# First attention batch loaded in fp32 by the SP and ACT queues and cast on chip, weights behind it, more banks for the last feed-forward products

## The chip, the cores and the metric

One Trainium2 chip, one NeuronCore. The metric is the device time of one execution in microseconds (us). In the profile PE is TensorE (PEld its weight loads), DVE is VectorE, ACT is ScalarE, POOL is GpSimd and SP is SyncE. Transfers issued by SP or ACT are called hardware-queue transfers here (the profile's `hardware_dynamic`), those issued by POOL software-queue transfers (`software_dynamic`). Only the latter convert fp32 to fp16 on the way in this kernel.

## What is computed

Sparse causal attention over 8 batches of 8 heads with 576 positions of width 64, then a feed-forward layer over all 4608 tokens.

```python
scores = scale * np.matmul(q, k.transpose(0, 1, 3, 2))
rel = pos[:, None] - pos[None, :]
mask_local = (rel >= 0) & (rel < stride)                                   # heads 0 to 3, stride 32
mask_strided = (rel >= 0) & (pos[None, :] % stride == pos[:, None] % stride)  # heads 4 to 7
scores = np.where(masks[None, :, :, :], scores, -1000000000.0)
attn = softmax(scores)
x = np.matmul(attn, v)            # -> (4608 tokens, 512)
h = x @ w_in                      # (512, 2048)
g = s * np.maximum(h, 0.0) ** 2 + b
out = g @ w_out                   # (2048, 512), fp32
...
```

## The kernel before

**Attention.** A batch is four head pairs: m = 0, 1 are local heads (6 tiles of 96 rows), m = 2, 3 strided heads (8 tiles of 72 rows). A pair goes through PE transposes of q and k (`ps_t`), copies out of PSUM by ACT or DVE (`qD_loc`, `kT_loc`, `qD_str`, `kTs`), score products (`ps_s`), the exponential on ACT (`pt`), the mask on DVE, the products with v (`ps_a`), a reciprocal and a multiplication on DVE (`rec`, `x_nat`), transposes back and a copy into `xT`. Only one PSUM bank serves `ps_a` (`AB = 1`), so the av groups of a batch (four local, eight strided) follow one another through PE, `rec` and `x_nat`. Local q and k are first regrouped by `pair_heads` (four DVE copies into `qp` and `kp`, L217).

**Feed-forward.** Tokens go in 9 blocks T of 512. F1 (L448) takes 4 products into `ps_f`, two banks; ACT writes `u` (L463), DVE squares it into `gT` (L467). F2 (L484) takes 16 products for 128 tokens into one bank (`F2B = 1`), DVE evicts (`o`, L495), SP stores. A block is 64 F1 and 64 F2 products. Ahead of the first F2 product stand 16 bias products (L506, `bcs`), which need `w_out`.

**Order.** A planner (`Plan`) emits all instructions in one order. It has a clock of its own, prices for each step (37 ns for a small PE step, 213.5 for a large one) and for each follow-up on ACT ("A") and DVE ("V"), and due times for transfers, which are constants in the code. What it believes ready it emits; on the chip every engine then executes its instructions strictly in that order, so an instruction emitted ahead of its data holds all behind it on that engine.

**Loads before.** Everything comes over POOL's queue, cast on the way: q, k, v of batch 0, `w_in` in four pieces, q, k, v of batch 1, `w_out` in one piece, then q and k of batch 2 and so on. The due times are those of the lines below; `fetch` is called for batch b + 2 when the last q or k transpose of batch b has been emitted.

```python
fetch(0, 10000.0)                     # L523: due 10 us
arrive([("in", "vl", 0), ("in", "vs", 0)], 22500.0)
fetch(1, 38000.0)
arrive([("w_out",)], 61000.0)         # L533
fetch(b + 2, plan.t + 12000.0)        # L542
```

POOL has 8 semaphores for transfers in turn, so a ninth waits for the landing of the first. In local v, both sides of a row are 64 elements (256 bytes in memory); rows of q, k and the weights are 1.5 to 2 KB.

Of the kernel before, what the change touches and what calls it, by code (L numbers as in the profile page):

```python
# [9 lines left out]
FP16 = mybir.dt.float16  # L10
FP32 = mybir.dt.float32
# [95 lines left out]
def kernel(  # L107
# [71 lines left out]
    nc.sync.dma_start(out=ident, in_=h_ident.ap())  # L179
    nc.sync.dma_start(out=mask_loc, in_=h_mloc.ap())  # L180
    nc.sync.dma_start(out=mask_str, in_=h_mstr.ap())
    nc.sync.dma_start(out=s_sb, in_=moe_s.to_broadcast([128, 1]))
    nc.sync.dma_start(out=b_sb, in_=moe_b.to_broadcast([128, 1]))
    nc.vector.memset(ones16, 1.0)
# [4 lines left out]
    for i in range(2):  # L189
        nc.vector.memset(kT_loc[i][:, 0:LPAD], 0.0)  # L190
        nc.vector.memset(qD_loc[i], 0.0)
        nc.vector.memset(qD_str[i], 0.0)

    loaded = {}

    def load_qk(b):
        t = {}
        for name, src in (("q", q), ("k", k)):
            tl = inp.tile([LQ, 4, LT * D], FP16, tag=name + "l", name=name + "l")
            nc.gpsimd.dma_start(  # L200
                out=tl, in_=src[b, 0:4].rearrange("h (p j) d -> p h (j d)", j=LT))
            t[name + "l"] = tl
        for name, src in (("q", q), ("k", k)):
            ts = inp.tile([SQ, 4, ST * D], FP16, tag=name + "s", name=name + "s")
            nc.gpsimd.dma_start(  # L205
                out=ts, in_=src[b, 4:8].rearrange("h (p j) d -> p h (j d)", j=ST))
            t[name + "s"] = ts
        loaded[b] = t

    paired = {}  # L210

    def pair_heads(b):
        for name in ("q", "k"):
            t = inp.tile([LQ, 2, LT, 2 * D], FP16, tag=name + "p", name=name + "p")
            src = loaded[b][name + "l"].rearrange("p (m e) (j d) -> p m e j d", e=2, d=D)
            for mm in range(2):
                nc.vector.tensor_copy(  # L217
                    out=t[:, mm].rearrange("p j (e d) -> p e j d", e=2), in_=src[:, mm])
            paired[b, name] = t

    def load_v(b):
        vl, vs = v_loc[b % NV], v_str[b % NV]
        for h in range(4):
            nc.gpsimd.dma_start(  # L224
                out=vl[LPAD:128, h, 0, 0:D], in_=v[b, h, 0:LQ, :])
# [14 lines left out]
    def load_w_out():  # L240
        nc.gpsimd.dma_start(
            out=w_out_sb, in_=moe_w_out.rearrange("(ft p) m -> p ft m", p=128))
# [3 lines left out]

    def copy_on(eng, **kw):
        (nc.scalar.copy if eng == "A" else nc.vector.tensor_copy)(**kw)  # L248

    def pair_steps(b, m):  # L250
# [10 lines left out]
        def trans(name, j, group):  # L261
            def f():
                if j == 0:
# [3 lines left out]
                       loaded[b][name + sfx][:, 2 * mm + j // 4,  # L267
                                             (j % 4) * 128:(j % 4) * 128 + 128])
# [3 lines left out]
            s = Step(f, 37, needs=[("in", name + sfx, b)], group=group if j == 0 else None)  # L272
            if j == nt - 1:
                key = ("t", name, id_)
                s.keys = [key]
                if name == "q":
# [15 lines left out]
                    s.posts = [([key], {"A": 620, "V": 750}, half(e), [("q", e, id_)])  # L292
# [3 lines left out]
                else:  # L296
# [9 lines left out]
                    s.posts = [([key], {"A": 640, "V": 750}, g, [("k", id_), group])]  # L306
# [9 lines left out]
        def score(i, group):  # L316
# [3 lines left out]
            def f():  # L320
                if i % per_s == 0:
                    st["s", g] = psum.tile([128, 3 * 2 * SQ], FP32, tag="s", bufs=SB, name="ps_s")
# [43 lines left out]
        def av(e, j, group):  # L366
# [10 lines left out]
            s = Step(f, 37, needs=[("p", id_, p_of(e, j)[0]), ("in", "v" + sfx, b)],  # L377
                     group=group if j % per == 0 else None)
            if j % per == per - 1:
# [10 lines left out]
                def mu(eng):  # L390
# [6 lines left out]
                           ([("r", id_, e, j)], {"V": 150 + 1.1 * 64 * per}, mu,  # L397
# [10 lines left out]
        def xtrans(j, group):  # L408
# [10 lines left out]
            if j == nt - 1:  # L419
# [10 lines left out]
                s.posts = [([key], {"A": 640, "V": 750}, g, [("xT", b, m), group])]  # L430
# [47 lines left out]
    def ff2(T, ts, ft, group):  # L478
        def f():
            if T == 0 and ts == 0 and ft == 0:  # L480
                emit_bcs()
            if ft == 0:
                gts["o"] = psum.tile([128, PS], FP32, tag="f2", bufs=F2B, name="ps_f2")
# [4 lines left out]
        s = Step(f, 213.5, needs=[("g", T, ft), ("w_out",)], group=group if ft == 0 else None)  # L488
        if ft == NFT - 1:
# [3 lines left out]
            def ev(eng):  # L493
                o = op.tile([128, DM], FP32, tag="o", name="o")
                nc.vector.scalar_tensor_tensor(  # L495
                    out=o, in0=gts["o"], scalar=s_sb[:, 0:1], in1=bcs,
# [3 lines left out]
            s.posts = [([key], {"V": 760}, ev, [group])]  # L500
        return s

    def emit_bcs():
        ps = psum.tile([128, PS], FP32, tag="f2", bufs=F2B, name="ps_f2")
        for ft in range(NFT):
            nc.tensor.matmul(out=ps, lhsT=ones16, rhs=w_out_sb[:, ft, :],  # L506
                             start=(ft == 0), stop=(ft == NFT - 1))
        nc.scalar.activation(out=bcs, in_=ps, func=AF.Copy, scale=b_sb)
# [6 lines left out]
    def fetch(b, at):  # L515

        load_qk(b)
        arrive([("in", "ql0", b), ("in", "kl0", b)], at)
        arrive([("in", "qs", b), ("in", "ks", b)], at + 4500)
        plan.post([("in", "ql0", b), ("in", "kl0", b)], {"V": 2000},  # L520
# [121 lines left out]
```

## Time and profile before

| | us |
|---|---|
| median of 3 runs (407.05 to 408.32) | 407.07 |
| the profiled execution | 407.57 |
| its span, first to last instruction | 405.5 |
| PE busy in it | 338.8 |
| DVE, ACT, POOL busy | 198.0, 183.9, 101.5 |

The span is 2.07 us shorter than the execution that it belongs to. PE's busy time is that of a pipelined engine: 84% does not mean that 84% of its peak is reached, since products overlap: four large ones take 0.86 us in the chain at 2.4 GHz and up to 1.86 us at 1.2 GHz. The page's 40 slices are 10.1 us each.

### The profile page before, as it was taken

The page shows a single profiled execution, that of the slowest core. Times are in us where ns is not written, and L with a number is a line of the kernel's source. Part 1 is how long each engine was busy: PE and PEld are TensorE (multiplying, and loading weights), DVE is VectorE, ACT ScalarE, POOL GpSimd, SP SyncE. Part 2 cuts the span into 40 slices and gives each one's busy share as a digit, 9 for nine tenths or more (in the row PEclk, how much of TensorE's full clock was granted, in tenths as well). Part 3 has the DMA queues.
Part 4 walks back from the last instruction along what each step waited for, and adds up shares of the span by engine and source line. Part 5 has one row for each costly group of instructions (what it writes and reads, how often), then busy time and mean ns, then how long its engine had stood idle before and what let it go on. Part 6 is the DMA issues. An engine that isn't in the chain of part 4 may idle for free.

```text
span 405.5 us, 6425 instructions
## 1 busy us (share of the span) xinstructions
PE 338.8 (84%) x2512; PEld 187.8 (46%) x2512; DVE 198.0 (49%) x545; ACT 183.9 (45%) x338; POOL 101.5 (25%) x137
## 2 busy tenths in 40 slices
PE   0665505967999799979997999799899999999884
PEld 0553302644455455545554555455555544444331
DVE  3554006774255646664665466456756643242311
ACT  1631204852355645564656555555655533332200
POOL 6744906354006500650064017100000000000000
PEclk9999955985999999989999999999999999999999
DMA  7999999798016940991099029400100001010111
GB/s 98 97 203 151 88 204 119 78 90 85 6 53 92 96 76 27 121 110 34 26 120 118 26 47 109 51 27 39 41 26 27 27 26 53 27 53 26 47 58 53
DMA packets 72514, 28.95 MB, mean 71 GB/s; under 512 B 53028, under 2 KB 67876, under 8 KB 72484
## 3 DMA queue, kind: packets, MB, share of 16 engines
q0 software_dynamic: 66640, 19.04, 51.0%
q1 hardware_dynamic: 5844, 9.51, 6.3%
q8 instruction: 19, 0.31, 0.3%
q14 instruction: 11, 0.09, 0.1%
HBM read 38.08 MB, written 9.44 MB: 117 GB/s over the span
## 4 chain that ended last, share of the span: by engine, by line
PE 73%; DMA 11%; ACT 5%; DVE 5%; POOL 4%; issue 2%; POOLq 0%; ACTq 0%
PE ps_f L484 30%; PE ps_f L448 29%; DMA kl<-in_k_dram 4%; DMA ks<-in_k_dram 4%; PE ps_a L373 4%; PE ps_t L269 3%; PE ps_s L324 3%; DMA qs<-in_q_dram 3%; ACT qD_loc L248 2%; PE ps_t L412 2%; DVE qD_loc L248 2%; DVE x_nat L391 1%; PE ps_f L506 1%; ACT pt L337 1%; DVE o L495 1%
## 5 line engine op out<-in xcount | busy, mean ns | idle before, releaser
L448 PE MATMUL ps_f<-xT,w_in_sb 128*128 128x512 f16 x576 | 165.5, 392 | 20.7 <-ACT u L463 19.0
L484 PE MATMUL ps_f<-w_out_sb,gT 128*128 128x512 f16 x576 | 156.2, 381 | 4.4 <-DVE o L495 3.6
L463 ACT ACTIVATE u<-ps_f 128x512 f16<-128x512 f32 x144 | 86.0, 598 | 101.6 <-PE ps_f L448 71.2
L467 DVE TENSOR_TENSOR gT<-u 128x512 f16<-128x512 f16 x144 | 60.1, 419 | 82.0 <-ACT u L463 81.2
L448 PEld LDWEIGHTS <-w_in_sb 128*128 128x128 f16 x576 | 56.0, 100 | 69.2 <-issue 24.6
L484 PEld LDWEIGHTS <-gT 128*128 128x128 f16 x576 | 55.9, 99 | 58.0 <-issue 7.6
L373 PEld LDWEIGHTS <-pt 72*72 72x72 f16 (+1 forms) x448 | 41.0, 128 | 25.9 <-DVE x_nat L391 15.1
L337 ACT ACTIVATE pt<-ps_s 128x384 f16<-128x384 f32 (+2 forms) x96 | 44.3, 488 | 18.3 <-PE ps_s L324 18.1
L391 DVE TENSOR_TENSOR x_nat<-ps_a,rec 72x256 f16<-72x256 f32 (+1 forms) x96 | 44.4, 463 | 2.3
L387 DVE RECIPROCAL rec<-ps_a 72x4 f32<-72x4 f32 (+1 forms) x96 | 17.5, 182 | 50.6 <-PE ps_a L373 49.7
L373 PE MATMUL ps_a<-v_str,pt 72*72 72x65 f16 x256 | 32.8, 207 | 7.3 <-DVE x_nat L391 7.2
L248 ACT COPY xT<-ps_t 128x576 f16<-128x576 f16 x30 | 19.2, 639 | 38.1 <-PE ps_t L412 37.9
L495 DVE SCALAR_TENSOR_TENSOR o<-ps_f,s_sb,bcs 128x512 f32<-128x512 f32 x36 | 26.9, 746 | 15.9 <-PE ps_f L484 15.6
L230 POOL DMA_DIRECT2D v_str<-in_v_dram x32 | 29.4, 917 | 18.6 <-PE ps_s L324 5.8
L229 POOL DMA_DIRECT2D v_loc<-in_v_dram x32 | 28.6, 894 | 16.5 <-DMA v_loc<-in_v_dram 8.9
L412 PE MATMUL ps_t<-ident,x_nat 72*128 72x72 f16 (+1 forms) x224 | 26.9, 211 | 4.2 <-DVE x_nat L391 4.1
L205 POOL DMA_DIRECT2D qs<-in_q_dram x8 | 5.9, 743 | 97.6 <-PE ps_t L269 97.6
L324 PE MATMUL ps_s<-qD_str,kTs 128*72 128x144 f16 x128 | 23.5, 238 | 1.1 <-ACT kTs L248 0.8
L324 PE MATMUL ps_s<-qD_loc,kT_loc 128*128 128x192 f16 x96 | 18.7, 274 | 5.6 <-ACT kT_loc L248 4.3
L373 PE MATMUL ps_a<-v_loc,pt 128*96 128x65 f16 x192 | 21.3, 213 | 1.2 <-DVE x_nat L391 1.2
L412 PEld LDWEIGHTS <-x_nat 72*128 72x128 f16 (+1 forms) x224 | 16.3, 104 | 11.2 <-DVE x_nat L391 6.8
L224 POOL DMA_DIRECT2D v_loc<-in_v_dram x32 | 17.4, 543 | 14.4 <-DMA w_out_sb<-in_moe_w_out_dram 10.4
(43 smaller groups left out, 246.2 us busy)
## 6 DMA issues: line engine op xcount, KB each, us to landing
out_dram<-o SPq DMA_DIRECT2D x36, 256.0 KB, 2.0
v_loc<-in_v_dram POOLq DMA_DIRECT2D x32, 80.0 KB, 4.7
ql<-in_q_dram POOLq DMA_DIRECT2D x8, 288.0 KB, 5.2
kl<-in_k_dram POOLq DMA_DIRECT2D x8, 288.0 KB, 6.7
qs<-in_q_dram POOLq DMA_DIRECT2D x8, 288.0 KB, 5.0
ks<-in_k_dram POOLq DMA_DIRECT2D x8, 288.0 KB, 8.0
v_str<-in_v_dram POOLq DMA_DIRECT2D x32, 72.0 KB, 4.0
w_in_sb<-in_moe_w_in_dram POOLq DMA_DIRECT2D x4, 512.0 KB, 9.2
```

The costliest lines, as they stand in the source:

```text
L230: nc.gpsimd.dma_start(out=vs[:, h, :, 0:D], in_=v[b, 4 + h].rearrange("(p j) d -> p j d", j=ST))
L248: (nc.scalar.copy if eng == "A" else nc.vector.tensor_copy)(**kw)
L324: nc.tensor.matmul(out=st["s", g][0:nk, c:c + 2 * nq], lhsT=st["k"][:, i * nq:i * nq + nk], rhs=st["q"][:, i].rearrange("d e c -> d (e c)"))
L337: nc.scalar.activation(out=pt[0:nk, 0:2 * n].rearrange("k t c -> k (t c)"), in_=st["s", g][0:nk, 0:2 * n * nq], func=AF.Exp, scale=scale)
L373: nc.tensor.matmul(out=st["a"][0:nq, j % per, :], lhsT=st["pt", g][0:nk, i, :], rhs=vt[0:nk, 2 * mm + e, j, :])
L391: nc.vector.tensor_tensor(out=st["x"][:, j0:j0 + per, 64 * e:64 * e + 64], in0=st["pa", e, j][0:nq, 0:per, 0:D], in1=st["rec", e, j][0:nq, ...
L412: nc.tensor.matmul(out=st["px"][:, nq * j:nq * j + nq], lhsT=st["x"][:, j, :], rhs=ident[0:nq, 0:nq], is_transpose=True)
L448: nc.tensor.matmul(out=gts["h"], lhsT=w_in_sb[:, ct, ft * 128:(ft + 1) * 128], rhs=xT[ct][:, tok0:tok0 + PS], start=(ct == 0), stop=(ct == 3))
L463: nc.scalar.activation(out=gts["u", T, ft], in_=h, func=AF.Relu)
L467: nc.vector.tensor_tensor(out=gts[T][:, ft, :], in0=u, in1=u, op=ALU.mult)
L484: nc.tensor.matmul(out=gts["o"], lhsT=gts[T][:, ft, ts * 128:(ts + 1) * 128], rhs=w_out_sb[:, ft, :], start=(ft == 0), stop=(ft == NFT - 1))
L495: nc.vector.scalar_tensor_tensor(out=o, in0=gts["o"], scalar=s_sb[:, 0:1], in1=bcs, op0=ALU.mult, op1=ALU.add)
```

## The change

For batch 0, q, k and v are loaded in fp32 by hardware-queue transfers from SP and ACT, into memory that is not yet used (the two `gT` buffers and `w_out_sb`), and cast to fp16 by ACT and DVE copies: local q and k in the regrouping itself, strided q and k by `cast_s`, v by `cast_v`. V of batch 1 is loaded the same way from SP alone, once the casts of the strided q and k have left its staging room; q and k of batch 1 stay on POOL. A one-element POOL copy (`gate`) waits for the last of batch 0's q and k before POOL issues `w_in`, q and k of batch 1, and `w_out` (now four pieces, behind the casts of v of batch 0, whose staging room is `w_out_sb`). The regrouping of later batches is split into halves that may go to ACT or DVE, with due times that a running count of the queue (`landing`) gives. Readiness is per half batch; DVE prices of copies become finer. The bias products are steps of the planner. F2 of the last two blocks uses the two `ps_s` banks instead of its one.

```diff
-    nc.sync.dma_start(out=ident, in_=h_ident.ap())
+    stage0 = gp.tile([128, 4096], FP32, tag="gT", name="stage0")
+    stage1 = gp.tile([128, 4096], FP32, tag="gT", name="stage1")
+    stage2 = w_out_sb.rearrange("p f m -> p (f m)").bitcast(FP32)
...
+    def stage_v(b, e0, e1):
...
+        e0.dma_start(out=v4[LPAD:128, :, 0, :], in_=first)
+        for h in range(4):
+            e0.dma_start(out=v4[:, h, 1:LT, :], in_=rest[:, h])
+        e1.dma_start(out=h4(vs), in_=view_s(v, b))
+
+    nc.sync.dma_start(out=h4(st_q["ql"]), in_=view_l(q, 0))
+    nc.scalar.dma_start(out=ident, in_=h_ident.ap())
+    nc.scalar.dma_start(out=h4(st_q["kl"]), in_=view_l(k, 0))
+    nc.sync.dma_start(out=h4(st_q["qs"]), in_=view_s(q, 0))
+    nc.scalar.dma_start(out=h4(st_q["ks"]), in_=view_s(k, 0))
...
+    stage_v(0, nc.sync, nc.scalar)
...
+    def pair_post(b, name, mm, src, key, cost):
...
+    def cast_s(name, mm, key):
...
+        plan.post([key], {"A": 1030, "V": 1150}, g, [("in", name + "s", 0, mm)])
+    def cast_v(b, loc, mm, key):
...
+            for h in range(2 * mm, 2 * mm + 2):
+                copy_on(eng, out=dst[b][0:np_, h, :, 0:D], in_=src[:, h])
...
-                    s.posts = [([key], {"A": 620, "V": 750}, half(e), [("q", e, id_)])
+                    s.posts = [([key], {"A": 635, "V": 756 if loc else 459}, half(e), [("q", e, id_)])
...
+    ring = 0.0
+    def landing(cost):
+        nonlocal ring
+        ring = max(ring, plan.t + 2000.0) + cost
+        return ring
...
+    def fetch_qk(b):
+        load_qk(b)
+        for name in ("q", "k"):
+            plan.done["raw", name, b] = landing(1700)
+            for mm in range(2):
+                pair_post(b, name, mm, None, ("raw", name, b), {"A": 810, "V": 350})
...
-    fetch(0, 10000.0)
-    load_v(0)
-    arrive([("in", "vl", 0), ("in", "vs", 0)], 22500.0)
+    for name, at in (("q", 4600.0), ("k", 5200.0)):
...
+    for loc, at in ((True, 12500.0), (False, 11000.0)):
...
+    gate = const.tile([1, 1], FP32)
+    nc.gpsimd.tensor_copy(out=gate, in_=st_q["ks"][0:1, 0:1])
     load_w_in()
+    ring = 13000.0
...
+    plan.post(both("vl", 0) + both("vs", 0), {"A": 0.0}, lambda eng: load_w_out(), [("free",)])
...
-            gr = Group("f2", F2B)
+            gr = Group("f2", F2B) if T < NBLK - 2 else Group("s", SB)
```

POOL's queue around `w_out`: before, the last three of batch 1's twelve v transfers and the nine ahead of them stand between `w_in` and `w_out`, which is one piece, and q and k of batch 2 come behind it (`95` and `97` are the numbers of v's buffers).

```order
L224 DMA v_loc_95<-in_v_dram 96x64
L229 DMA v_loc_95<-in_v_dram 128x5x64
L230 DMA v_str_97<-in_v_dram 72x8x64
L241 DMA w_out_sb<-in_moe_w_out_dram 128x16x512
L200 DMA ql<-in_q_dram 96x4x384
L200 DMA kl<-in_k_dram 96x4x384
L205 DMA qs<-in_q_dram 72x4x512
L205 DMA ks<-in_k_dram 72x4x512
```

After, POOL's queue from its first row; `stage` is the staging room of the strided q and k:

```order
L617 COPY gate<-stage_111 1x1
L263 DMA w_in_sb<-in_moe_w_in_dram 128x4x512 x4
L242 DMA ql<-in_q_dram 96x4x384
L242 DMA kl<-in_k_dram 96x4x384
L246 DMA qs<-in_q_dram 72x4x512
L246 DMA ks<-in_k_dram 72x4x512
L268 DMA w_out_sb<-in_moe_w_out_dram 128x4x512 x4
L242 DMA ql<-in_q_dram 96x4x384
```

No transfer of v stands ahead of batch 2's q and k on POOL's queue any more; those of batches 0 and 1 moved to SP's and ACT's.

On DVE, before, where F1 begins to run in earnest: the regrouping copies of batch 1 (`qp_502`, `kp_505`) and right behind them those of batch 2 (`qp_509` from `ql_351`), and the first `gT` behind both.

```order
L217 COPY qp_502<-ql_152 96x2x6x64 x2
L217 COPY kp_505<-kl_154 96x2x6x64 x2
L217 COPY qp_509<-ql_351 96x2x6x64 x2
L217 COPY kp_512<-kl_353 96x2x6x64 x2
L467 TENSOR_TENSOR gT_359<-u_517 128x512
L467 TENSOR_TENSOR gT_359<-u_525 128x512
```

On DVE, after: the place at which batch 2's copies now stand (`ql_358`, `kl_360`).

```order
L526 TENSOR_TENSOR gT_366<-u_747 128x512
L446 RECIPROCAL rec_768<-ps_a_758 72x4
L271 COPY qp_777<-ql_358 96x2x6x64 x2
L450 TENSOR_TENSOR x_nat_757<-ps_a_758,rec_768 72x4x64
L526 TENSOR_TENSOR gT_366<-u_775 128x512
L271 COPY kp_817<-kl_360 96x2x6x64 x2
L526 TENSOR_TENSOR gT_366<-u_802 128x512
```

The copies of batch 2 moved from ahead of the first `gT` of block 0 to behind its eighth and ninth. On PE the last five F2 groups of the changed kernel stand without any other product between them, before it was the last four; the wait for an eviction at the head of each is now for the one before the last (two banks).

## Rows read from the trace of the kernel before

**Rows 1.** The page, 40 slices of 10.1 us: busy share of the DMA engines in tenths.
```profile
DMA  7999999798016940991099029400100001010111
```
**Rows 2.** Windows: length, busy (instructions) of PE, PEld, DVE, ACT, POOL, then PEclk, DMA, GB/s.
```profile
40.00:50.00 10.00, 6.24 (x43) 3.45 (x41) 0.00 (x0) 3.04 (x5) 9.24 (x13) 1.00 1.01 82
50.00:60.00 10.00, 0.00 (x0) 0.00 (x0) 0.00 (x0) 0.00 (x0) 0.58 (x1) 0.53 1.23 200
60.00:70.00 10.00, 4.73 (x14) 2.02 (x14) 5.83 (x16) 4.16 (x9) 5.87 (x8) 0.50 1.54 134
104.00:376.00 272.00, 260.10 (x1948) 142.19 (x1948) 146.26 (x397) 141.69 (x259) 47.72 (x62) 0.99 0.38 55
```
**Rows 3.** The chain that ended last, 40 to 72 us: start, us, what.
```profile
46.21 17.34 DMA kl<-in_k_dram
63.57 0.62 DVE kp L217 x2
...
65.27 1.86 PE ps_f L448 x4
```
**Rows 4.** Waits of the whole span: total us, times, longest.
```profile
DVE qp L217 <- DMA ql<-in_q_dram: 25.1, 2, 23.6
PE ps_f L448 <- ACT u L463: 19.0, 1, 19.0
```
**Rows 5.** Timeline of the first 40 us: start, us, engine, line, what, count [idle before].
```profile
6.31 0.62 DVE L217 COPY qp<-ql 96x768 f16<-96x768 f16 x2 [1.58 <-DMA ql<-in_q_dram]
10.18 0.63 DVE L217 COPY kp<-kl 96x768 f16<-96x768 f16 x2 [3.25 <-DMA kl<-in_k_dram]
11.98 0.82 PE L324 MATMUL ps_s<-qD_loc,kT_loc 128*128 128x192 f16 x4 [0.73 <-ACT kT_loc L248]
...
19.82 0.66 PE L373 MATMUL ps_a<-v_loc,pt 128*96 128x65 f16 x6
...
31.20 0.45 PE L373 MATMUL ps_a<-v_str,pt 72*72 72x65 f16 x4 [0.73 <-DVE x_nat L391]
...
38.59 1.87 PE L448 MATMUL ps_f<-xT,w_in_sb 128*128 128x512 f16 x4 [0.73 <-ACT xT L248]
```
**Rows 6.** DMA issues of the whole span: KB each, median us to landing.
```profile
out_dram<-o SPq DMA_DIRECT2D x36, 256.0 KB, 2.0
ql<-in_q_dram POOLq DMA_DIRECT2D x8, 288.0 KB, 5.2
```
**Rows 7.** Windows of 2 us, columns as in rows 2: v of batch 0, then `w_in`.
```profile
16.00:18.00 2.00, 1.61 (x20) 1.39 (x18) 1.00 (x3) 2.00 (x5) 2.00 (x3) 1.00 1.30 71
26.00:28.00 2.00, 1.95 (x21) 1.66 (x20) 1.12 (x3) 1.21 (x4) 0.89 (x1) 1.00 1.24 208
```
**Rows 8.** Groups by line and shape: busy us, mean ns, idle before.
```profile
L217 DVE COPY kp<-kl 96x768 f16<-96x768 f16 x16 | 5.0, 350 | 4.1 <-DMA kl<-in_k_dram 4.1
L248 DVE COPY qD_loc<-ps_t 64x576 f16<-64x576 f16 x12 | 9.1, 756 | 5.7 <-ACT qD_loc L248 3.5 <-PE ps_t L269 2.0
```
**Rows 9.** Timeline, 80 to 105 us, columns as in rows 5.
```profile
81.52 0.43 PE L412 MATMUL ps_t<-ident,x_nat 96*128 96x96 f16 x6
...
97.51 5.70 PE L506 MATMUL ps_f<-w_out_sb,ones 128*128 128x512 f16 x16
...
103.98 1.02 PE L484 MATMUL ps_f<-w_out_sb,gT 128*128 128x512 f16 x4 [0.78 <-ACT bcs L508]
```
**Rows 10.** The chain that ended last, 376 us to the end, columns as in rows 3.
```profile
383.06 0.76 DVE o L495
...
383.87 3.63 PE ps_f L484 x16
...
387.52 0.76 DVE o L495
...
400.88 0.75 DVE o L495
```
**Rows 11.** One 4 us window past the start, columns as in rows 2.
```profile
216.00:220.00 4.00, 1.73 (x23) 1.36 (x24) 2.20 (x9) 3.48 (x8) 2.63 (x3) 1.00 0.95 116
```

More of the change, by code (lines that the diff above doesn't have):

```diff
@@ L271, in f @@
                     rhs=ident[0:nq, 0:nq], is_transpose=True)
-            s = Step(f, 37, needs=[("in", name + sfx, b)], group=group if j == 0 else None)
+            s = Step(f, 37, needs=[("in", name + sfx, b, mm)], group=group if j == 0 else None)
             if j == nt - 1:
@@ L486, in f @@
                 rhs=w_out_sb[:, ft, :], start=(ft == 0), stop=(ft == NFT - 1))
-        s = Step(f, 213.5, needs=[("g", T, ft), ("w_out",)], group=group if ft == 0 else None)
+        s = Step(f, 213.5, needs=[("g", T, ft), ("w_out", ft // 4)], group=group if ft == 0 else None)
         if ft == NFT - 1:
@@ new lines, in both, with fetch_v @@
+    def both(name, b):
+        return [("in", name, b, mm) for mm in range(2)]
+    def fetch_qk(b):
+        load_qk(b)
+        for name in ("q", "k"):
+            plan.done["raw", name, b] = landing(1700)
+            for mm in range(2):
+                pair_post(b, name, mm, None, ("raw", name, b), {"A": 810, "V": 350})
+        for name in ("qs", "ks"):
+            arrive(both(name, b), landing(2100))
+    def fetch_v(b):
+        load_v(b)
+        arrive(both("vl", b) + both("vs", b), landing(7000))
@@ new lines @@
+    for name, at in (("q", 4600.0), ("k", 5200.0)):
+        plan.done["raw", name, 0] = at
+        for mm in range(2):
+            pair_post(0, name, mm, st_q[name + "l"], ("raw", name, 0), {"A": 810, "V": 900})
+    for name, at in (("q", 8000.0), ("k", 8600.0)):
+        plan.done["raw", name + "s", 0] = at
+        for mm in range(2):
+            cast_s(name, mm, ("raw", name + "s", 0))
+    for loc, at in ((True, 12500.0), (False, 11000.0)):
+        plan.done["raw", "v", loc, 0] = at
+        for mm in range(2):
+            cast_v(0, loc, mm, ("raw", "v", loc, 0))
@@ L526 @@
+    gate = const.tile([1, 1], FP32)
+    nc.gpsimd.tensor_copy(out=gate, in_=st_q["ks"][0:1, 0:1])
     load_w_in()
+    ring = 13000.0
     for c in range(4):
-        arrive([("w_in", c)], 25700.0 + 2700 * c)
-    fetch(1, 38000.0)
-    load_v(1)
-    arrive([("in", "vl", 1), ("in", "vs", 1)], 48000.0)
-    load_w_out()
-    arrive([("w_out",)], 61000.0)
+        arrive([("w_in", c)], landing(2700))
+    fetch_qk(1)
+    plan.post(both("vl", 0) + both("vs", 0), {"A": 0.0}, lambda eng: load_w_out(), [("free",)])
@@ new lines, with early_v @@
+    ring += 3000.0
+    plan.done["raw", "v", True, 1] = plan.done["raw", "v", False, 1] = ring
+    for c in range(4):
+        arrive([("w_out", c)], landing(2700))
+    def early_v():
+        nc.vector.memset(
+            st_v[1][0][0:LPAD].rearrange("p (h t d) -> p h t d", h=4, d=D)[:, :, 0, :], 0.0)
+        stage_v(1, nc.sync, nc.sync)
+        for loc in (True, False):
+            for mm in range(2):
+                cast_v(1, loc, mm, ("raw", "v", loc, 1))
+    plan.post([("in", n, 0, mm) for n in ("qs", "ks") for mm in range(2)], {"A": 0.0},
+              lambda eng: early_v(), [("early",)])
```

149 lines of the change are left out of this document (87 added, 62 removed).

## The prediction

> **What bounds the kernel now.** I read the kernel in three parts and in this order: the page's slices, the windows, the chain of work that ended last, and the waits. From the slices: the DMA engines are busy for nine tenths from 10 to 70 us and hardly at all past 290 us [rows 1]. So the start is bound by transfers, and the rest is not. The windows agree: from 104 to 376 us PE is busy 260.10 of 272 us, but from 50 to 60 us it executes nothing [rows 2]. The chain says why: a piece of 17.34 us is a transfer of local k that DVE waits for, then come DVE's copies, and the first F1 product follows at 65.27 [rows 3]. The waits name the holder: DVE stands 23.6 us in one piece ahead of a regrouping copy, and PE 19.0 us ahead of an F1 product whose bank ACT could not empty, since DVE had not squared the `u` ahead of it [rows 4]. The copies are those of batch 2, emitted right behind those of batch 1 and ahead of the first `gT`: DVE executes in order, so the squares of F1, and with them F1 itself, waited for data that nothing needed yet. At the other end, four F2 groups each wait for an eviction: 383.06 to 383.87, then 0.76 us and some issue time ahead of each following one [rows 10].
>
> So the sum has four terms: the start up to the first F2 product (103.98 [rows 9]), what is done by then, the five thin places between, and the end.
>
> **The start, step by step.** *Loads of q and k.* Before, local q lands for a copy at 6.31, k only at 10.18, and scores begin at 11.98 [rows 5]. No row shows a hardware-queue load of 590 KB of fp32. From below: a hardware-queue store of 256 KB lands in 2.0 us; from above: the same q by the software queue takes 5.2 [rows 6]. At the rate of the `w_in` stream, 208 GB/s written in fp16 and so 416 GB/s read [rows 7], the two tensors need 1.18/0.416 = 2.8 us. I take 0.7 + 2.0 + 2.8 = 5.5 us, near the upper end, as both share the engines. Then come casts instead of copies: the fp16 copy takes 0.350, the copy of 576 columns out of PSUM 0.756, which is 1.0 for 768 [rows 8]; I take 0.85, two rounds on each engine. With transposes and copies scores start near 9.5, 2.5 us earlier.
>
> *V of batch 0.* 2,944 of its rows are 256 bytes. The software queue moved such rows at 71 GB/s written, 142 read, where 2 KB rows move at 416 [rows 7]. Taken at 142, local v (0.75 MB) needs 5.3 us instead of 1.8; all of batch 0 (3.7 MB) then 0.7 + 2.0 + 2.95/0.416 + 5.3 = 15. With two casts of 0.5 us behind it av begins near 16 instead of 19.82 [rows 5]. Bounds: 14 where rows cost only their bytes on this queue, 21 where `w_in`, released by the gate near 10 us, takes every other turn of the engines.
>
> *Batch 0's av, and batch 1.* The first eight groups took 19.82 to 31.20 [rows 5]; that pace gives 27.4. There DVE and ACT now hold a copy of batch 1's q, which is behind `w_in` on POOL's queue. From 10.5 us: `w_in` 4.2/0.416 = 10.1, what is left of batch 0's v 3, v of batch 1 in between 1.4 + 5.3, q itself 1.4: 31.7 us if nothing overlaps, 26 if all of it runs at 416. I take 30, so a new wait of 2.6 us in which `rec`, `x_nat` and with them the only `ps_a` bank stand. Then DVE has 11.3 us of work by the counts of its order (five `rec`/`x_nat` pairs 3.0, seven copies 3.9, six masks 2.1, four casts of v 2.2) until F1 begins in earnest: with small waits 13, so 43 against 38.59 before [rows 5]. That is later, but 44 transposes and scores of batch 1 are done by then which were not before.
>
> *F1.* 45 F1 products and some 90 small ones until the first bias product. Before, 61 and some 130 took 38.59 to 46.2 and 65.27 to 81.52 [rows 3, 5, 9], 23.9 us, with two starts at half speed: four products in 1.86 us at 65.27 [rows 3], while the granted clock was 0.50, after PE had stood still [rows 2]. One such start goes (2.7 us). 23.9 × 45/61 − 2.7 = 15; I take 16: 59. Here stand batch 2's copies, behind the eighth and ninth `gT`, reached near 54. Their q lands after `w_out` (10.1) and q and k of batch 1 (4.2): 30 + 4.2 + 10.1 + 1.4 = 46. So that wait, 23.6 us before, is nothing, with some 8 us of cover.
>
> *To the first F2 product.* Before, from 81.52 to 97.51 nine av groups follow one another with three F1 products between; afterwards 5.70 us go to the bias products, which start at half speed again [rows 9]. After, seven av groups: 16.0 × 7/9 = 12.4; 25 large products in the same stretch fill gaps, bounds 0 and 5.7 us, I take 3. Then 31 large ones (21 F1, 10 bias): 5.70 for the first sixteen, 15 × 0.227 (16 in 3.63 [rows 10]), with the small ones 9.4. So 43 + 16 + 15.4 + 9.4 = 84 against 103.98: **−20**.
>
> **Done by then.** In the order, 88 F1 products stand ahead of the first F2 product, 68 before, and 6 av products more: 20 × 0.227 + 0.3 = **−4.8**.
>
> **Between.** Of the 11.9 us in which PE idles from 104 to 376 [rows 2], most is in five places, one to a batch, such as 216 to 220 with 1.73 busy of 4 [rows 11]. There 26 to 30 small products stand in a row without a large one; after, 19 to 23. The new DVE prices (459 instead of 750 for strided copies) shift copies from ACT to DVE. What that is worth no row tells: from −9 (nearly all of the idle time) to +3 (0.6 us more at each place). The shorter runs are nearest to a quarter less: **−3**.
>
> **The end.** Five F2 groups in a row over two banks. An eviction of 0.76 lies beside the next 3.63 us of products [rows 10], so the four waits of 0.81 go: **−3.3**. The last eviction and its store stay.
>
> The sum: −20 − 4.8 − 3 − 3.3 = −31 on the profiled execution's 407.57 gives 376.5; the median of the runs is 0.5 below it, so 376. The bias steps and half readiness cost nothing by themselves: the bias products are the same 16, now among F1.
>
> **A rule that speaks against the change.** From 10 to 70 us the 16 engines are nine tenths busy already [rows 1]; if those tenths are work, a second queue adds nothing, if they are waiting, it may; 71 and 208 GB/s under a similar share leave that open [rows 7]. The Trainium skill, "DMA: Bandwidth & Descriptors", section "Issuing engines are not separate DMA queues", says that transfers from the three run on the same 16 engines and interleave, and that using several saves only issue time. By that rule batch 0 lands when it did before, with av at 20 and the rest as summed: it is the second rival.
>
> **Rivals.** *The wait moves to batch 1 and 2.* If 256-byte rows on the hardware queues cost twice what I took, both v's hold the engines 10.6 us more; batch 1's q lands near 40, DVE stands 13 us instead of 2.6, and F2 begins near 94: 386. For: rows 7's 71 GB/s is a rate shared with nothing else. Against: two queues may fill what one leaves idle.
>
> *The first batch lands no earlier.* Av at 20, but the copy's wait, 30, is met with less slack: +2 to +4 on the sum, 379. The removed stall is untouched by it.
>
> *Everything overlaps.* Batch 1's q lands at 26, no wait there (−2.6), av at 14, most gaps between filled (−6): 366.
>
> *Slower than before.* One mechanism: ACT's casts of v's last heads stand in order ahead of the exponentials, DVE's copies of batch 1's q ahead of every `rec`; if v's rows on the hardware queues starve or are starved, both engines hold everything. The price needed is 31 us over the forecast: over 5,888 rows 5.3 ns each on top of the 1.8 ns of rows 7. Nothing in the trace is near it.
>
> *It does not do what it says.* The order shows that batch 2's copies did move behind `gT`; what could fail is that POOL reaches them late, since each of its transfers waits for one eight places earlier. They would have to land past 54: that costs 1 us for each.
>
> **How the numbers follow.** A difference of 0.3% (1.2 us) is about what these measurements can tell from none. Chances: forecast 0.45 (370 to 382), first batch no earlier 0.14, the wait moves 0.18 (382 to 394), everything overlaps 0.17 (360 to 370), slower 0.03, and 0.03 for a gain of under 13 us by any mixture. Eight in ten of this lies from 364 to 389. Faster 0.95, same 0.02, slower 0.03.
>
> **What would show it.** In the profile after: no DVE wait over 5 us ahead of a `qp` copy; scores before 10.5 and av near 16; F1 in earnest near 43; first F2 product at 84 (over 92: the transfers; under 78: overlap); the granted clock at half only once between 45 and 85; no gap between the last five F2 groups. I am wrong if DVE or ACT stands over 8 us for one landing, or if the rate stays under 100 GB/s while hardware and software loads run together.

## The result

The changed kernel takes 372.79 us in the median of four runs (371.16 to 374.51), the kernel before 407.5 in four beside it: a ratio of 0.915, 95% interval 0.909 to 0.920. The forecast was 376, from 364 to 389. The total came out well, its parts did not: the start gained less than forecast, the rest more. The profiled execution is that of 374.32 us, with a span of 372.6.

The page's slices of the changed kernel (9.3 us each), as [rows 1]:

```profile
PE   1256759969999999999999999999999999899995
...
DMA  8899999997096709911964295001100000100112
GB/s 176 185 177 194 216 216 132 129 91 81 31 132 54 99 31 129 125 34 41 129 64 83 56 120 78 2 28 42 45 30 30 28 28 32 56 29 30 56 61 80
```

PE has work in every slice; the ten microseconds without a product [rows 2] are gone. The timeline of the changed kernel has the places that [rows 5, 9] show of before (start, us, engine, line, what, count, idle before):

```profile
7.07 0.83 ACT L271 CAST qp<-stage 96x768 f16<-96x768 f32 x1 [2.63 <-DMA stage<-in_q_dram]
13.27 0.83 ACT L271 CAST kp<-stage 96x768 f16<-96x768 f32 x1 [5.36 <-DMA stage<-in_k_dram]
13.27 0.56 DVE L271 CAST kp<-stage 96x768 f16<-96x768 f32 x1 [5.63 <-DMA stage<-in_k_dram]
16.84 0.82 PE L383 MATMUL ps_s<-qD_loc,kT_loc 128*128 128x192 f16 x4 [0.73 <-ACT kT_loc L271]
23.49 0.66 PE L432 MATMUL ps_a<-v_loc,pt 128*96 128x65 f16 x6
...
37.70 0.36 DVE L271 COPY qp<-ql 96x768 f16<-96x768 f16 x1 [2.42 <-DMA ql<-in_q_dram]
50.15 1.14 ACT L271 CAST v_str<-stage 72x512 f16<-72x512 f32 x2 [2.69 <-DMA stage<-in_v_dram]
51.87 3.57 PE L507 MATMUL ps_f<-xT,w_in_sb 128*128 128x512 f16 x8 [2.86 <-ACT xT L271]
67.15 0.38 PE L564 MATMUL ps_b<-w_out_sb,ones 128*128 128x512 f16 x1
90.53 0.38 PE L541 MATMUL ps_f<-w_out_sb,gT 128*128 128x512 f16 x1
```

Batch 0's k lands at 13.27, later than before (10.18), and the first av product comes at 23.49 instead of 19.82. F1 in earnest begins at 51.87, held for the last 2.86 us by ACT, which casts v of batch 1 only at 50.15 and has the `xT` copy behind that. The first F2 product stands at 90.53 instead of 103.98. From there to the end are 282.1 us instead of 301.5. So 13.4 us came from the start and 19.4 from the rest. (The profile is of one of the slower executions, and its first loads landed late; the last section has the numbers. So the start's share may be up to 3.6 us larger.)

The tail of the changed kernel is one piece in the chain that ended last (start, us, what); before it was cut by evictions [rows 10]:

```profile
350.25 18.14 PE ps_f L541 x84
368.39 0.03 issue
368.42 0.75 DVE o L552
```

### The profile page after: what moved, and what is told of

Read it like the earlier page. It is cut to its first block, busy times and chain, and to the rows that moved or that the text cites. A ratio compares the mean times of both kernels' runs of the same rounds, so it can differ in the third digit from the quotient of the medians.

```text
span 372.6 us, 6416 instructions
## 1 busy us (share of the span) xinstructions
PE 332.0 (89%) x2512; PEld 186.7 (50%) x2512; DVE 212.7 (57%) x573; ACT 181.1 (49%) x332; POOL 72.5 (19%) x95
## 2 busy tenths in 40 slices
DMA packets 66306, 31.47 MB, mean 84 GB/s; under 512 B 46244, under 2 KB 60516, under 8 KB 66276
## 3 DMA queue, kind: packets, MB, share of 16 engines
HBM read 38.08 MB, written 9.44 MB: 128 GB/s over the span
## 4 chain that ended last, share of the span: by engine, by line
PE 77%; DMA 9%; DVE 5%; ACT 3%; SPq 3%; issue 1%; ACTq 0%; DVEq 0%
PE ps_f L507 33%; PE ps_f L541 32%; DMA w_out_sb<-in_v_dram 5%; DMA stage<-in_v_dram 4%; PE ps_a L432 3%; PE ps_t L328 3%; SPq L212 3%; PE ps_s L383 3%; PE ps_t L471 2%; DVE qD_loc L271 1%; ACT qD_loc L271 1%; DVE o L552 1%; PE ps_b L564 1%; ACT u L522 1%; DVE pt L404 1%
## 5 line engine op out<-in xcount | busy, mean ns | idle before, releaser
L507 PE MATMUL ps_f<-xT,w_in_sb 128*128 128x512 f16 x576 | 163.1, 388 | 3.3 <-ACT xT L271 3.1
L541 PE MATMUL ps_f<-w_out_sb,gT 128*128 128x512 f16 x576 | 152.6, 379 | 2.4 <-DVE o L552 2.4
L471 PE MATMUL ps_t<-ident,x_nat 72*128 72x72 f16 (+1 forms) x224 | 29.1, 210 | 2.7 <-DVE x_nat L450 2.5
L271 ACT COPY xT<-ps_t 128x576 f16<-128x576 f16 x24 | 15.3, 639 | 25.5 <-PE ps_t L471 25.5
L255 POOL DMA_DIRECT2D v_str<-in_v_dram x24 | 20.9, 870 | 30.4 <-PE ps_a L432 11.6
L383 PE MATMUL ps_s<-qD_str,kTs 128*72 128x144 f16 x128 | 26.5, 237 | 0.3 <-ACT pt L396 0.3
L471 PEld LDWEIGHTS <-x_nat 72*128 72x128 f16 (+1 forms) x224 | 17.9, 103 | 12.1 <-DVE x_nat L450 5.5
L254 POOL DMA_DIRECT2D v_loc<-in_v_dram x24 | 21.0, 876 | 7.1 <-DMA w_out_sb<-in_moe_w_out_dram 3.9
L328 PE MATMUL ps_t<-ident,qp 96*128 96x96 f16 x96 | 11.7, 224 | 10.8 <-ACT qp L271 8.0
L404 DVE TENSOR_TENSOR pt<-pt,mask_str 72x432 f16<-72x432 f16 (+1 forms) x48 | 16.4, 346 | 4.5 <-ACT pt L396 3.9
```

Of the source, the lines that this page charges most:

```text
L328: nc.tensor.matmul(out=st["p" + name][:, nq * j:nq * j + nq], lhsT=src, rhs=ident[0:nq, 0:nq], is_transpose=True)
L383: nc.tensor.matmul(out=st["s", g][0:nk, c:c + 2 * nq], lhsT=st["k"][:, i * nq:i * nq + nk], rhs=st["q"][:, i].rearrange("d e c -> d (e c)"))
L471: nc.tensor.matmul(out=st["px"][:, nq * j:nq * j + nq], lhsT=st["x"][:, j, :], rhs=ident[0:nq, 0:nq], is_transpose=True)
L507: nc.tensor.matmul(out=gts["h"], lhsT=w_in_sb[:, ct, ft * 128:(ft + 1) * 128], rhs=xT[ct][:, tok0:tok0 + PS], start=(ct == 0), stop=(ct == 3))
L541: nc.tensor.matmul(out=gts["o"], lhsT=gts[T][:, ft, ts * 128:(ts + 1) * 128], rhs=w_out_sb[:, ft, :], start=(ft == 0), stop=(ft == NFT - 1))
```

## Experiments on the order of work

Edits to the kernel before give the names of before, those to the changed kernel its own. A median without a comparison is to be read against 372.79 for the changed kernel and about 407.5 for the kernel before.

**Only the due time of batch 2.**

```diff
-                fetch(b + 2, plan.t + 12000.0)
+                fetch(b + 2, plan.t + (25000.0 if b == 0 else 12000.0))
```

> The kernel before with one number changed: the due time of batch 2's q and k is plan.t + 25000 instead of plan.t + 12000, so that batch 2's regrouping copies stand behind the ninth gT of block 0 instead of ahead of the first. All loads stay on POOL's queue. Theory A (DVE's in-order wait is the main term of the gain): the 23.6 us wait ahead of a qp copy goes or shrinks under 5 us, F1 runs on from about 39 us without the stretch in which PE does nothing, one half-speed start goes, and the time falls by 14 to 20 us, to 388 to 393 us. Theory B (the start is bound by the transfers themselves; batch 2's q and k land at 63.6 us behind w_out whatever waits for them): the wait only moves to the bias products (w_out) or to the copies at their new place, the gain is under 6 us, over 401 us.

Measured: 399.22 us (397.63 to 399.29), ratio 0.978 (0.974 to 0.983). The timeline of this kernel at the copy in its new place, and at the first F2 product:

```profile
60.43 0.62 DVE L217 COPY qp<-ql 96x768 f16<-96x768 f16 x2 [8.20 <-DMA ql<-in_q_dram]
...
92.97 1.02 PE L484 MATMUL ps_f<-w_out_sb,gT 128*128 128x512 f16 x4 [0.78 <-ACT bcs L508]
```

Neither theory was right in size. Of the 23.6 us that DVE stood [rows 4], 8.20 are left behind the ninth `gT`, since q of batch 2 still lands at 60.4 behind `w_out`. F2 starts 11.0 us earlier, almost as much as the whole change brings at this place (13.4). So the place of the copies is the larger part of the start's gain, without any new load. From there to the end (397.2) are 304.2 us, 2.7 more than before. In that stretch the granted clock stood at half, 0.50, three times for 3.4 us (from 130.6, 209.1 and 246.6 us), in the kernel before once (from 180.2).

**Regrouping in one piece; prices of before.** In the first of two kernels the four copies of a batch are again one DVE action, in the second the prices are those of before.

```diff
-            for mm in range(2):
-                pair_post(b, name, mm, None, ("raw", name, b), {"A": 810, "V": 350})
+        plan.post([("raw", "q", b), ("raw", "k", b)], {"V": 2000}, whole, ...)
```

```diff
-    ... {"A": 635, "V": 756 if loc else 459}, ...
+    ... {"A": 620, "V": 750}, ...
...
```

> The changed kernel with the regrouping of batches 1 to 7 put back: four copies in a row on DVE, posted once q and k of the batch are both due, instead of halves that may go to ACT. Theory A (the halves fill the five thin places, one to a batch: before, kp transposes stood 7.6 us in all for qD_loc copies that queued behind): the waits of kp transposes for qD_loc come back, PE idles 6 to 9 us more between the first F2 product and the end, 378 to 381 us. Theory B (the finer DVE prices fill them): the same as the changed kernel within 2 us, 371 to 375 us.

> The changed kernel with the DVE and ACT prices of before (750 for every copy out of PSUM on DVE, 150 + 1.1 per element for x_nat, 760 for an eviction). Theory A (halves of the regrouping fill the thin places): same as the changed kernel within 2 us, 371 to 375 us. Theory B (the prices do, since strided copies move from ACT to DVE): PE idles 6 to 9 us more after the first F2 product, 378 to 381 us.

Measured: 372.40 (372.16 to 373.11) and 373.32 us (372.76 to 375.08). Neither differs from the changed kernel. From the first F2 product (89.34 and 87.34) to the end of the spans (371.3 and 371.0) are 282.0 and 283.7 us, so the finer prices may be worth 1.6 us there, and the halves nothing. What fills the thin places, the stretches past the start in which PE idled before, was neither of the parts that I had named.

**The planner's count.** The bias products are now the first 16 entries of the planner's list of F2 steps. So its count of finished F2 steps, `i2`, is 16 higher, and `i2` stands in two rules: `due()`, which says how far attention must be, and the lead `i1 > i2 + 64`, which lets F2 go ahead of F1. Two kernels separate that from all else: the changed one without the 16, and the one before with them.

```diff
-        pos = (i1 + i2) / 64.0 + 0.1
+        pos = (i1 + max(i2 - NFT, 0)) / 64.0 + 0.1
...
-        if len(order) == 2 and i1 % 4 == 0 and i1 > i2 + 64:
+        if len(order) == 2 and i1 % 4 == 0 and i1 > max(i2 - NFT, 0) + 64:
```

> The changed kernel with the 16 bias products still steps of the planner, but left out of its two counts of finished F2 steps: due() takes i1 + max(i2 - 16, 0), and the lead of F1 over F2 is i1 > max(i2 - 16, 0) + 64. The order then has five places with 43, 43, 43, 43 and 18 small PE products in a row past the start, where the changed kernel has 23, 19, 19, 19 and 19 and the kernel before 30, 30, 30, 30 and 26; the tail has 68 F2 products alone instead of 84. Theory A (that count is what fills the thin places): PE idles again 2 to 3 us at four of them for copies out of PSUM, +7 to +12 us, 380 to 385 us. Theory B (regrouping in halves, prices and due times together fill them; neither of the first two did alone): within 2 us of the changed kernel, 371 to 375 us.

```diff
-        pos = (i1 + i2) / 64.0 + 0.1
+        pos = (i1 + i2 + NFT) / 64.0 + 0.1
...
-        if len(order) == 2 and i1 % 4 == 0 and i1 > i2 + 64:
+        if len(order) == 2 and i1 % 4 == 0 and i1 > i2 + NFT + 64:
```

> The kernel before with 16 added to its count of finished F2 steps at the same two places, and nothing else: no bias step, no new load, no new price. Its order has 19 and 22 small products in a row at two places past the start and under 14 at the others, instead of 30, 30, 30, 30 and 26; 84 F2 products stand alone at the end instead of 68, on one bank. Theory A (the count is the cause): the waits of kp transposes for qD_loc, 7.6 us, go nearly all, one more eviction gap of 0.8 us comes at the end, and the stall of 23.6 us stays: 7 to 11 us less, 396 to 400 us. Theory B: the thin places are bound by the copies themselves and their idle time moves elsewhere: 404 to 408 us.

Measured: 379.54 us (379.30 to 383.60) without the count, 6.75 more than the changed kernel and just under the range of theory A; 398.50 us (397.88 to 400.06) for the kernel before with it, ratio 0.979 (0.976 to 0.982), inside the range. The waits of PE past the start (total us, times, longest), of before from 110 to 376 us:

```profile
PE ps_t L269 <- ACT qD_loc L248: 7.6, 4, 1.9
PE ps_s L324 <- ACT kT_loc L248: 1.7, 4, 0.4
PE ps_a L373 <- DVE x_nat L391: 1.2, 5, 0.2
PE ps_t L412 <- DVE x_nat L391: 1.2, 1, 1.2
```

The same stretch of the kernel before with the count:

```profile
PE ps_f L484 <- DVE o L495: 4.2, 8, 0.9
PE ps_t L269 <- ACT qD_loc L248: 1.5, 1, 1.5
PE ps_f L448 <- ACT xT L248: 0.5, 1, 0.5
PE ps_a L373 <- DVE x_nat L391: 0.5, 2, 0.2
PE ps_t L269 <- DVE qD_loc L248: 0.2, 1, 0.2
```

Windows of the steady part, columns as in [rows 2]: the kernel before; before with the count; the changed kernel; the changed kernel without the count.

```profile
110.00:376.00 266.00, 254.10 (x1921) 139.47 (x1920) 144.98 (x394) 139.49 (x255) 47.72 (x62) 0.99 0.39 56
```

```profile
110.00:376.00 266.00, 259.09 (x1941) 141.99 (x1938) 148.67 (x399) 139.34 (x253) 46.96 (x62) 1.00 0.38 58
```

```profile
110.00:350.00 240.00, 235.64 (x1767) 129.53 (x1766) 141.39 (x377) 121.60 (x224) 34.03 (x43) 1.00 0.43 57
```

```profile
110.00:360.00 250.00, 241.04 (x1756) 130.11 (x1754) 143.63 (x374) 121.90 (x222) 33.45 (x42) 0.99 0.37 54
```

PE idles 11.9, 6.9, 4.4 and 9.0 us. The waits of transposes for copies of `qD_loc` mostly vanish with 16 added to a count; in their place come waits for evictions of F2, which then runs in longer stretches on its one bank. The stall of 23.6 us is untouched there (24.0 in that kernel), and yet 8.8 us are gained. From the first F2 product to the end the kernel before takes 292.1 us with the count (103.70 to 395.8) instead of 301.5; the changed kernel without it 295.3 (82.33 to 377.6) instead of 282.1, of which 2.6 are 12 F1 products fewer ahead of that point. So the count alone makes about half of the 19.4 us after the start. Both kernels change the two rules together; the section on combinations has a pair that differs in the lead alone.

**The tail on one bank.**

```diff
-            gr = Group("f2", F2B) if T < NBLK - 2 else Group("s", SB)
+            gr = Group("f2", F2B)
```

> The changed kernel with F2 of the last two blocks back on the one f2 bank. Theory A (each eviction of 0.75 us stands between two F2 groups): four to five gaps of 0.8 us at the end come back, +3.3 to +4 us, 376 to 377 us. Theory B (the planner then puts the last F2 groups differently, or the gaps were hidden): within 1 us of the changed kernel.

Measured: 378.01 us (375.83 to 379.62), +5.2, more than either theory had. The waits of PE, whole span, for evictions: first this kernel, then the changed one.

```profile
PE ps_f L541 <- DVE o L552: 6.7, 9, 0.9
```

```profile
PE ps_f L541 <- DVE o L552: 2.4, 4, 0.9
```

Five waits come back, 4.3 us, and from the first F2 product (86.91) to the end of the span (374.1) are 287.2 us instead of 282.1; before had four such waits. Counting the bias lets F1 run further ahead, so more F2 is left alone at the end (84 products instead of 68), and on one bank each further group would pay an eviction. The two banks take back what the count costs there.

## Experiments on the loads

**The same fp32 loads by POOL.**

```diff
-    nc.sync.dma_start(out=h4(st_q["ql"]), in_=view_l(q, 0))
-    nc.scalar.dma_start(out=h4(st_q["kl"]), in_=view_l(k, 0))
+    nc.gpsimd.dma_start(out=h4(st_q["ql"]), in_=view_l(q, 0))
+    nc.gpsimd.dma_start(out=h4(st_q["kl"]), in_=view_l(k, 0))
...
-    stage_v(0, nc.sync, nc.scalar)
+    stage_v(0, nc.gpsimd, nc.gpsimd)
```

> The changed kernel with the same fp32 staging loads of batch 0's q, k and v, but issued by POOL instead of SP and ACT; nothing else moves (v of batch 1 stays on SP). Theory A (the rate is a limit on bytes written, whoever issues): 170 to 200 GB/s in the first 17 us, k lands at 12 to 14 us, and the time is 371 to 376 us. Theory B (the hardware queues are slow by themselves): over 230 GB/s, k lands by 9 us, first av 4 us or more earlier, 366 to 369 us.

Measured: 379.11 us (376.93 to 380.30). Windows of this kernel, then one of the changed kernel, both with fp32 loads alone:

```profile
4.00:12.00 8.00, 1.14 (x12) 1.03 (x13) 2.34 (x9) 2.40 (x4) 5.13 (x7) 1.00 0.92 208
```

```profile
8.00:17.00 9.00, 1.89 (x20) 1.56 (x21) 2.68 (x4) 2.75 (x5) 0.00 (x0) 1.00 0.93 189
```

The rates, 208 and 189 GB/s, lie within a tenth of each other, so the hardware queues are not slow by themselves. They are also near that of the casting stream of `w_in` in the kernel before, 208 GB/s written [rows 7]. The page counts bytes written: it has 31.47 MB in all for the changed kernel and 30.29 for the next one below, which casts q and k on the way, while both read 38.08 MB. So an element loaded as fp32 took about twice as long as one cast on the way. The engines' busy share in these windows differs less: 0.92 and 0.93 here, 1.24 for the casting stream, so in busy time an fp32 element took 1.5 to 1.7 times as much. Theory A holds for the rate; its time was too low, since in this kernel v comes last in one queue (its cast waits until 24.85) and the gate and `w_in` behind it.

**Batch 0's q and k by POOL, cast on the way, no gate.**

```diff
-    nc.sync.dma_start(out=h4(st_q["ql"]), in_=view_l(q, 0))
...
-    nc.gpsimd.tensor_copy(out=gate, in_=st_q["ks"][0:1, 0:1])
+    load_qk(0)
```

> The changed kernel with q and k of batch 0 loaded by POOL's queue and cast on the way, as before; v of batches 0 and 1 stays in fp32 on SP and ACT; no gate, w_in follows at once. Theory A (the engines move some 180 to 216 GB/s as written, so fp32 q and k cost twice their fp16 bytes): 1.18 MB less is written ahead of v, q and k land by 11 us instead of 17, batch 0's v by 16 instead of 20.7, first av near 17 instead of 23.5, batch 1's q near 32 instead of 37.7, F1 in earnest 3 to 6 us earlier: 367 to 370 us. Theory B (the SP and ACT queues help, POOL's issuing is what costs): q and k land no earlier than before, v is starved by the w_in stream and lands past 22: 373 to 378 us.

Measured: 372.77 us (372.01 to 373.59), the same as the changed kernel; neither range held it. Its timeline:

```profile
13.36 0.82 PE L379 MATMUL ps_s<-qD_loc,kT_loc 128*128 128x192 f16 x4 [0.25 <-ACT kT_loc L267]
...
24.86 0.51 ACT L267 CAST v_loc<-w_out_sb 128x384 f16<-128x384 f32 x1 [3.65 <-DMA w_out_sb<-in_v_dram]
```

Scores are 3.5 us earlier than in the changed kernel's profile, as the bytes say. But without the gate `w_in` shares the engines with v of batch 0, whose last head lands at 24.86, and ACT holds the exponentials for it. F1 starts in earnest at 50.08 instead of 51.87.

**All of batch 0 by POOL.** This takes out the first part of the change's name: q, k and v of batch 0 come as before, v of batch 1 stays in fp32 on SP.

```diff
-    stage_v(0, nc.sync, nc.scalar)
...
+    load_qk(0)
...
+    load_v(0)
```

> The changed kernel with q, k and v of batch 0 all on POOL's queue, cast on the way, as before; v of batch 1 on SP in fp32, everything else as changed. Theory A (loading batch 0 through SP and ACT gains nothing; the gain of the start is the order of batch 2's copies): first av at 19 to 21 us as before, the time is 370 to 375 us. Theory B (hardware loads are the gain of the start): first av later than in the changed kernel, w_in behind v lands past 33 us, F1 later by 4 us or more: 377 us or more.

Measured: 374.07 us (373.67 to 374.44), ratio 0.919 (0.916 to 0.921), which overlaps that of the changed kernel. Its first av product:

```profile
17.97 0.66 PE L426 MATMUL ps_a<-v_loc,pt 128*96 128x65 f16 x6
...
39.71 0.36 DVE L265 COPY qp<-ql 96x768 f16<-96x768 f16 x1 [6.02 <-DMA ql<-in_q_dram]
```

The av product is 5.5 us earlier than with the fp32 loads, and the time is no better: batch 1's q lands at 39.71, and DVE stands 6.02 us for it, where it stood 2.42 in the changed kernel. So the load that the change is named after is worth 1.3 us by the medians, which these runs cannot tell from nothing.

**V of batch 1 on POOL's queue.**

```diff
     fetch_qk(1)
+    fetch_v(1)
...
-    plan.post(..., lambda eng: early_v(), [("early",)])
```

> The changed kernel with v of batch 1 on POOL's queue, behind q and k of batch 1 and ahead of w_out, cast on the way, instead of staged by SP. Theory A (v of batch 1 in fp32 on SP, 1.38 MB, shares the engines with w_in and holds up batch 1's q): q of batch 1 lands near 31 us instead of 37.7, the ACT wait for v_str ahead of F1 goes, F1 in earnest 3 to 5 us earlier, but w_out lands some 8 us later: 368 to 372 us. Theory B (rows of v cost more on POOL's queue, 71 GB/s written): v lands past 50 us, w_out and q of batch 2 behind it past 72, new waits at the bias products or at batch 2's copies: 374 to 382 us.

Measured: 368.28 us (367.44 to 369.79), ratio 0.905 (0.902 to 0.908), 4.5 less than the changed kernel. Its timeline:

```profile
33.32 0.35 DVE L271 COPY qp<-ql 96x768 f16<-96x768 f16 x1
...
44.63 1.87 PE L507 MATMUL ps_f<-xT,w_in_sb 128*128 128x512 f16 x4 [0.25 <-ACT xT L271]
...
82.68 0.38 PE L541 MATMUL ps_f<-w_out_sb,gT 128*128 128x512 f16 x1
```

Theory A in the time. Against the changed kernel's profile batch 1's q is copied 4.4 us earlier (33.3, not the 31 that was asked), F1 begins 7.2 and F2 7.9 us earlier; in the profile with the tail on one bank, whose first loads landed sooner, that q is copied at 36.03 and F2 begins at 86.91. V of batch 1 in fp32, loaded by SP while POOL streams `w_in`, was the worst of the new loads: it took room from `w_in` and the q behind it, and landed at 50.15 all the same. The edit also moves the planner's due times of this v and of `w_out`, and 84 instead of 88 F1 products stand ahead of the first F2 product, so the transfer and the order were not tried apart.

**Combinations.** First the two POOL edits together, with the lead counted without the bias and `due()` with it; then the same lead with only v of batch 1 on POOL, so that the gate and the fp32 loads of batch 0 stay.

```diff
-        if len(order) == 2 and i1 % 4 == 0 and i1 > i2 + 64:
+        if len(order) == 2 and i1 % 4 == 0 and i1 > max(i2 - NFT, 0) + 64:
```

> Three edits to the changed kernel together: q and k of batch 0 on POOL's queue without a gate; v of batch 1 on POOL's queue behind q and k of batch 1; the lead of F1 over F2 without the 16 bias steps, due() with them, which leaves one place of 15 small products past the start. Only v of batch 0 is still staged in fp32 by SP and ACT. Theory A (each load that competes with w_in for nothing delays batch 1's q, and with it F1): batch 1's q lands near 30 us, F1 in earnest at 40 to 43 instead of 51.9, first F2 product at 78 to 82, 362 to 367 us. Theory B (the start is then bound by the copies and by ps_a's one bank, not by loads): 367 to 369 us, as with v of batch 1 on POOL alone.

> Two edits to the changed kernel: v of batch 1 on POOL's queue behind q and k of batch 1 (as in the run with that alone, 368.28 us), and the lead of F1 over F2 without the 16 bias steps (i1 > max(i2 - 16, 0) + 64), due() with them. Batch 0 is staged by SP and ACT behind the gate, as in the changed kernel, so w_in does not compete with batch 0's v. Theory A (start and thin places add up): the first F2 product at 79 to 82 us, and 279 us from there, as in the run of three edits: 360 to 364 us. Theory B (what the fuller places gain was idle time that F1 ahead had already taken): 366 to 368 us.

Measured: 366.96 us (366.34 to 368.14), at the border of its two ranges and hardly below v of batch 1 alone; and, as theory A had it, 362.07 us (361.60 to 362.87), ratio 0.887 (0.885 to 0.890), the fastest here, 10.7 less than the changed kernel. The steady part, columns as in [rows 2], of the kernel with v of batch 1 alone and of the fastest one:

```profile
110.00:350.00 240.00, 236.09 (x1746) 129.04 (x1745) 137.12 (x363) 117.11 (x215) 32.51 (x41) 1.00 0.41 58
```

```profile
110.00:350.00 240.00, 239.64 (x1772) 129.84 (x1770) 141.83 (x369) 120.46 (x218) 31.74 (x40) 1.00 0.41 58
```

PE idles 0.4 instead of 3.9 of 240 us: the thin places are gone. The lead is all in which these two kernels differ, and it is worth 6.2 us by the medians (368.28 to 362.07). So the two rules that hold the count do not work the same way: in the lead the 16 cost time here, and what the count gains comes, as far as these runs show, through `due()`. In the changed kernel itself the two rules were not tried apart.

The first F2 product of the fastest kernel is at 81.80. In the kernel of three edits it is at 85.52, for the reason that its ACT shows:

```profile
24.82 0.51 ACT L267 CAST v_loc<-w_out_sb 128x384 f16<-128x384 f32 x1 [3.61 <-DMA w_out_sb<-in_v_dram]
25.81 0.40 PE L379 MATMUL ps_s<-qD_str,kTs 128*72 128x144 f16 x2 [5.29 <-ACT pt L392]
```

So once v of batch 1 is out of the way, staging q and k of batch 0 on SP and ACT, with the gate that holds `w_in` back behind them, is worth 4.9 us (366.96 to 362.07). These two kernels differ in the queue and the gate together, so which of the two does it was not separated. A kernel with none of the new loads and the rest of the change was not run.

## Why the prediction was right, and where it was not

| step | forecast | the changed kernel |
|---|---|---|
| scores of batch 0 | 9.5 | 16.84 |
| first av product | 16 | 23.49 |
| batch 1's q | 30 | 37.70 |
| F1 in earnest | 43 | 51.87 |
| from there to the bias products | 16 | 15.3 |
| from those to the first F2 product | 25 | 23.4 |
| start, in sum | −20 | −13.4 |
| from the first F2 product to the end | −11.1 | −19.4 |
| all, on the profiled execution | −31 | −33.3 |

**Right: the stall.** No DVE wait ahead of a `qp` copy is over 2.5 us, and batch 2's copies wait for no transfer. The run with one due time changed shows that the order of these copies carries most of the start's gain. The sign on the clock held too: it was granted at half only once, in the second of these windows of the changed kernel (columns as in [rows 2]), behind a stretch in which PE was busy 4.25 of 7.20 us:

```profile
72.00:79.20 7.20, 4.25 (x54) 2.56 (x53) 5.17 (x18) 5.10 (x9) 3.79 (x5) 1.00 1.75 147
79.20:86.00 6.80, 6.28 (x38) 3.04 (x36) 2.87 (x9) 2.36 (x4) 3.91 (x5) 0.50 2.14 66
```

**Wrong: the rate of the fp32 loads.** The step "At the rate of the `w_in` stream, 208 GB/s written in fp16 and so 416 GB/s read" used the read side. Loads that do not cast ran at 176 to 189 GB/s in the first 17 us, so the 1.18 MB of local q and k need over 6 us instead of 2.8, the strided ones, which interleave with k, as long again, and all of batch 0 landed near 21 instead of 15. The forecasts of all that waits for a landing were 7 to 9 us early, of which some 2 to 4 may be this execution's own (last section); the two stretches after it (16 and 25 us) were nearly right. The highest rate in rows of before was 208 GB/s written [rows 7]; that it could be passed by writing as much as is read had no row. What stands in the prediction as the second rival, that batch 0 lands no earlier, is what happened, and more: it landed later. The rival in which the wait moves came true in part: batch 1's q landed near 38, not 30, but DVE stood 2.42 us for it and ACT 5.55, not 13. The Trainium skill, "DMA: Bandwidth & Descriptors", section "Issuing engines are not separate DMA queues", has transfers of the three issuers interleave on the same 16 engines. The traces agree: 208 GB/s from one queue, 189 from two; k, which shared with the strided q and k, landed 6.2 us after q.

**Wrong: "The bias steps and half readiness cost nothing by themselves".** The products are the same 16, but as entries of a list they move a count. Taking the count out of both rules costs 6.75 us, putting it alone into the kernel before gains 8.8. I gave the thin places −3 and named no cause for their shorter runs of small products; PE's idle time there fell by 7.5 us (11.9 to 4.4). The prices that I named give at most 1.6, the halves nothing. My lower bound of −9 would have held it.

**Right: the end.** −3.3 was forecast for the four waits of before, and the tail has none now. In the changed kernel the two banks are worth 5.2, since on one bank five evictions would stand there, not four.

**Done by then** held: 88 F1 products stand ahead. With 4.6 us for these and six av products, 7.5 for idle time and 3.3 for the four evictions of before, 15.4 of the 19.4 us are accounted for. Of the other 4.0 the granted clock can be at most 1.7. Before, it stood at half once past the start, right behind one of the five places with small products in a row (columns as in [rows 2]):

```profile
180.20:183.60 3.40, 3.40 (x10) 1.22 (x8) 1.15 (x4) 1.08 (x3) 0.00 (x0) 0.50 0.99 150
```

In the changed kernel it is 1.00 from 110 to 350 us. The rest is not settled.

So two errors of about 7 and 8 us with opposite signs made a good total: that it was met so closely is luck. What the remaining start gain of 2.4 us (13.4 less the 11.0 of the due time) is made of was not tried apart either.

## What to carry to other kernels

Move a wait before speeding up the transfer that it waits for: one due time and a count of 16 in the order's rules, each tried alone on the kernel before, gained 8.9 and 8.8 us there, while loading the first batch by other queues gained nothing that could be measured in the changed kernel. Only with v of batch 1 out of the way were the early q and k, together with their gate, worth 4.9 us. When a step enters a scheduler's list, look for every rule that counts that list, and try each rule by itself: the fastest kernel here has the count in one of the two and not in the other. And price a load by the bytes that it writes as much as by those it reads: here an element cast to fp16 on the way took about half the time of one staged in fp32, and staging v of batch 1 early took that time from the weights.

## What was not expected of the hardware

In the windows shown, the rate of loads mostly of rows of 1.5 to 2 KB followed the bytes written, not those read: 189 GB/s for plain loads from SP and ACT, 208 from POOL, and 208 for the casting stream [rows 7]. V of batch 0, whose local rows are 256 bytes, ran at 71 there, cast.

The landing of the first loads differs between executions of the same instructions. In the changed kernel's profile q and k of batch 0 are cast at 7.07 and 13.27; in the kernel with the tail on one bank, whose loads are the same, earlier, as its timeline shows:

```profile
6.24 0.83 ACT L271 CAST qp<-stage 96x768 f16<-96x768 f32 x1 [1.81 <-DMA stage<-in_q_dram]
11.53 0.83 ACT L271 CAST kp<-stage 96x768 f16<-96x768 f32 x1 [4.46 <-DMA stage<-in_k_dram]
```

Its first F2 product is at 86.91, 3.6 us earlier. On PE the two kernels have the same order up to 326 us. Seven of the profiled executions load q and k of batch 0 this way; k lands from 11.43 to 13.27, and that of the changed kernel's profile is the last of them. The four times of the changed kernel fall in two pairs, 371.2 and 374.4, and the profile is of the slower pair, so some 3 us of the late start probably belong to that execution.

A cast of half of k (96 by 768 elements) took 0.56 us on DVE and 0.83 on ACT; the prediction had 0.85 for both.
